# Tile loads issued from GpSimd's software DMA queue instead of SyncE's hardware queue

## The chip, the cores and the metric

The kernel runs on one core of one Trainium2 chip. The metric is device time in microseconds (us), as the median of several executions. Engines are named as in the profile: PE (TensorE), DVE (VectorE), ACT (ScalarE), POOL (GpSimd), SP (SyncE). A trailing q, as in SPq, is an engine's sequencer.

"The Trainium skill" is a set of notes on the chip. Where the text rests on it, it gives the page's title and section, and says whether the traces agree.

## The reference

Two independent decode attentions, A and B, each with 8 sequences, 32 heads, 4096 cached positions and head size 128, in bf16:

```python
def _A_ref(x, k_cache, v_cache, wq, wo):          # B is the same on its own inputs
    q = (x @ wq).reshape(8, 1, 32, 128).transpose(0, 2, 1, 3)
    scores = jnp.einsum("bhqd,bhkd->bhqk", q, k_cache) * (128 ** -0.5)
    p = softmax(scores, axis=-1)
    o = jnp.einsum("bhqk,bhkd->bhqd", p, v_cache)
    return o.transpose(0, 2, 1, 3).reshape(8, 1, 4096) @ wo
# result: concatenate([A, B], axis=-1)
```

There is one query per sequence, so every byte of the K and V caches is read once and used once: 1107 MB in all, with the weights.

## The kernel before

The work goes in 64 rounds, each over eight heads of one sequence: one K tile and one V tile of 8.39 MB each (128 partitions x 64 KB). Three such tiles fit in the on-chip memory: two slots take turns for K, the third holds V; the weights use the same slots at the start and the end. A load may be issued when the tile before it in its slot has been used.

```python
plan = [("wq", 0, 1), ("k", 0, 0), ("wq", 1, 2)]           # kind, number, slot
for n in range(NQ - 1):
    plan.append(("k", n + 1, (n + 1) % 2))
    plan.append(("v", n, 2))
plan += [("v", NQ - 1, NQ % 2), ("wo", 0, 2), ("wo", 1, (NQ - 1) % 2)]
...
def dma(out_ap, in_ap, key, deps, eng="sp"):               # loads go to SyncE
    return add(eng, lambda e: e.dma_start(out_ap, in_ap), deps, dma_key=key)
...
def load_tiles():
    while issued[0] < len(plan):
        kind, n, w = plan[issued[0]]
        prev = before[issued[0]]                           # the tile that held this slot
        dep = opUse.get(prev)                              # its last use, on PE
        if prev is not None and dep is None:
            return
        to, key = ring[:, w, :], ("t", w)
        if kind in ("k", "v"):
            ...
            opT[(kind, n)] = dma(to, from_, key, [dep])
        ...
        issued[0] += 1
```

In each quarter of a round, DVE multiplies a quarter of the K tile by the broadcast query, in place, and folds the halves of the head dimension. PE sums on, and DVE reduces the rest from PSUM:

```python
def make_mul(s):
    n = s // NR
    v = chunk(s).rearrange("p (t d) -> p t d", d=Dh)
    opMul[s] = add("dve", lambda e: e.tensor_tensor(
        v, v, qbc[:, n % 2, :].unsqueeze(1).to_broadcast([128, CT, Dh]), ALU.mult), [opT[("k", n)], opQbc[n]])
def make_fold(s):
    v = chunk(s).rearrange("p (t d) -> p t d", d=Dh)
    return add("dve", lambda e: e.tensor_tensor(v[:, :, 0:64], v[:, :, 0:64], v[:, :, 64:128], ALU.add), [opMul[s]])
```

The product with V of a round (`pv`, on PE) is done in the last two quarters of the following round; when it has ended, the next V load may be issued. The K slot comes free at the end of a round. GpSimd builds a few constants at the start (an identity, masks) and then does nothing.

Of the kernel before, what the change touches and what calls it, by code (L numbers as in the profile page):

```python
# [5 lines left out]
ALU = mybir.AluOpType  # L6
AX = mybir.AxisListType
# [24 lines left out]
class _Program:  # L32
# [11 lines left out]
    def add(self, eng, emit, deps=(), dma_key=None, moves=False):  # L44
        op = _Op(eng, emit, list(deps), dma_key, moves)
        if dma_key is not None:
            self.counts[dma_key] = self.counts.get(dma_key, 0) + 16
            op.token = (dma_key, self.counts[dma_key])
        for d in op.deps:
            if not (d.eng == "pe" and eng == "pe"):  # L50
                d.sig = True
        self.ops[eng].append(op)
        return op
# [86 lines left out]
def _build_kernel(nc, caches, out):  # L140
    B, Sq, D = caches[0][0].shape
    _, H, Sk, Dh = caches[0][1].shape
    NC = len(caches)
    assert B == 8 and Sq == 1 and Dh == 128 and Sk == 4096 and D == 1024 and H % 8 == 0 and 128 % H == 0
    DC = D // 128
    scale = float(Dh) ** -0.5
    HQ = 8
    MP = 128 // HQ
# [7 lines left out]
    PH = 128 // H  # L156
# [5 lines left out]
    with es:  # L162
# [5 lines left out]
        ident = sb("ident", [128, 128], BF16)  # L168
        own_m = sb("own_m", [128, HQ, PH], FP32)
        own_h = sb("own_h", [128, HQ], BF16)  # L170
        half = sb("half", [128, 2], FP32)
        E = sb("E", [128, 4, MB + PH - 1], BF16)
# [22 lines left out]
        proj = ps("proj")  # L195
# [10 lines left out]
        add = P.add  # L206

        def dma(out_ap, in_ap, key, deps, eng="sp"):
            return add(eng, lambda e: e.dma_start(out_ap, in_ap), deps, dma_key=key)


        def pool_select(view, base, pattern, dep, op=ALU.not_equal, fill=1.0, step=1):
            return add("pool", lambda e: e.affine_select(out=view, in_=view, compare_op=op, fill=fill,
                                                         base=base, pattern=pattern, channel_multiplier=step), [dep])
        c_ident = pool_select(ident[:], 0, [[-1, 128]], add("pool", lambda e: e.memset(ident[:], 0.0)))


        c_own = add("pool", lambda e: e.memset(own_m[:], 1.0))
        c_own = pool_select(own_m[:], 0, [[-MP, HQ], [0, PH]], c_own, ALU.is_ge, 0.0)
        c_own = pool_select(own_m[:], MP - 1, [[MP, HQ], [0, PH]], c_own, ALU.is_ge, 0.0, -1)  # L220
        own = own_m[:, :, 0]

        c_E = add("pool", lambda e: e.memset(E[:], 0.0))
        for q in range(4):
            c_E = pool_select(E[:, :, PH - 1:].rearrange("p i (j u) -> p i j u", u=PH)[:, :, :, 0], -32 * q, [[-8, 4], [-1, HQ]], c_E)
        c_oh = add("dve", lambda e: e.tensor_copy(own_h[:], own), [c_own])
        c_half = add("dve", lambda e: e.tensor_reduce(half[:], own.rearrange("p (g i) -> p i g", i=2), AX.X, ALU.add), [c_own])
        c_half = add("dve", lambda e: e.tensor_scalar(half[:], half[:], 1e30, -1e30, ALU.mult, ALU.add), [c_half])
        c_proj = add("dve", lambda e: e.memset(proj[:], 0.0))

        opT, opMul, opEacc, opRed, opNgm, opExp = {}, {}, {}, {}, {}, {}
        opPV, opAcc, opExt, opSt, opQb, opQbc, opQ, opQs, opQT = {}, {}, {}, {}, {}, {}, {}, {}, {}
        opOc, opNorm, opProj, opUse, opPM, opEv = {}, {}, {}, {}, {}, {}
        outs = []


        plan = [("wq", 0, 1), ("k", 0, 0), ("wq", 1, 2)]
        for n in range(NQ - 1):
# [11 lines left out]
        def where(n):  # L250

            return n // (B * HB), n // HB % B, n % HB
# [4 lines left out]
# [3 lines that stand above are left out]
                prev = before[issued[0]]  # L260
                dep = opUse.get(prev)
# [3 lines that stand above are left out]
                if kind in ("k", "v"):  # L265
                    c, b, hb = where(n)
                    from_ = caches[c][1 if kind == "k" else 2][b, hb * HQ:(hb + 1) * HQ].rearrange("u (m t) d -> (u m) (t d)", m=MP)
                    opT[(kind, n)] = dma(to, from_, key, [dep])
                elif kind == "wq":
                    opT[(kind, n)] = dma(to[:, 0:DC * H * Dh], caches[n][3].rearrange("(p k) n -> p (k n)", k=DC), key, [dep])  # L270
                else:
                    from_ = caches[n][4].rearrange("(p r) n -> p (r n)", r=H)
                    for i, (r0, r1) in enumerate(wo_cuts if n == NC - 1 else ((0, H),)):
                        opT[(kind, n, i)] = dma(to[:, r0 * D:r1 * D], from_[:, r0 * D:r1 * D], key if n < NC - 1 else ("w", i), [dep])
                issued[0] += 1


        def make_q(c):
            w = tile_of("wq", c)
            for f in range(2):  # L280
                def emit(e, f=f):
                    for k in range(DC):
                        for hb in range(HB):
                            col = k * H * Dh + (2 * hb + f) * 512
                            i = e.matmul(q_ps[f][32 * hb:32 * hb + B, :], xT[:, (c * DC + k) * B:(c * DC + k + 1) * B],  # L285
                                         w[:, col:col + 512], start=(k == 0), stop=(k == DC - 1), tile_position=(0, 32 * hb))
                    return i
                opQ[(c, f)] = add("pe", emit, [c_xT, opT[("wq", c)]] + [opQs.get((c - 1, hb, f)) for hb in range(HB)])
                for hb in range(HB):
                    rows = slice(32 * hb, 32 * hb + B)  # L290
                    opQs[(c, hb, f)] = add("act", lambda e, rows=rows, f=f: e.activation(q_sb[rows, c, f * 512:(f + 1) * 512], q_ps[f][rows, :], ACTF.Copy),  # L291
                                           [opQ[(c, f)]])
            opUse[("wq", c)] = opQ[(c, 1)]
# [153 lines left out]
        def emit_xT(e):  # L447
# [5 lines left out]
            return i  # L453
        op_xT = opUse[("x", 0)] = add("pe", emit_xT, [c_ident, op_x[-1]])
        load_tiles()
        c_xT = add("dve", lambda e: e.tensor_copy(xT[:], misc_bf16[:, 0:NC * DC * B]), [op_xT])
        make_q(0)
# [5 lines left out]
        for n in range(NQ):  # L463
            P.mark(n)
            for r in range(NR):
                s = n * NR + r
                make_mul(s)
                if s >= LAG:
                    make_red(s - LAG)
                if r == LAG - 1 and n >= 1:  # L470
                    make_shift(n - 1)
                fold = make_fold(s)
                if r == LAG - 1 and n >= 1:
                    make_pm(n - 1)
                if n == 0 and r == 1:
                    for c in range(1, NC):
                        make_q(c)
                        make_qT(c)
                if r == 2 and n >= 1:
                    make_pv(n - 1, 0, RG // 2)  # L480
                if r == 3 and n >= 1:
                    make_pv(n - 1, RG // 2, RG)
                    make_acc(n - 1)
                if r == 2 and n + 1 < NQ:
                    make_stage(n + 1)
                    make_qbc(n + 1)
                make_eacc(s, fold)
                load_tiles()
                if r == 3 and n >= 1:
                    make_ext(n - 1)  # L490
        P.mark(NQ)
        n = NQ - 1
# [4 lines left out]
        make_pv(n, 0, RG)  # L497
        make_acc(n)
        load_tiles()
        make_ext(n)  # L500
        make_norm(1)
# [31 lines left out]
def bass_concat_heads__mha_block_cached__mha_block_cached__decode_kernel(  # L533
    nc, A_x, A_k_cache, A_v_cache, A_wq, A_wo, B_x, B_k_cache, B_v_cache, B_wq, B_wo, out,
):
    caches = [(A_x, A_k_cache, A_v_cache, A_wq, A_wo), (B_x, B_k_cache, B_v_cache, B_wq, B_wo)]
    _build_kernel(nc, caches, out)
# [28 lines left out]
```

## Time and profile before

| before | value | view |
|---|---|---|
| time | 2566.66 us (3 runs), 2567.07 us with a fourth | runs |
| DMA share and rate, 500 to 2000 us | 1.00, 434 GB/s | windows |
| DVE busy | 85% of the span | page, part 1 |
| DVE idle per round, waiting for K | 4.8 us | waits |
| issue to landing, K and V | 40 us and 27.9 us | DMA issues |

The first fence is the windows view. Its columns are the stretch, its length, the busy time of PE, weight loads, DVE, ACT and POOL with instruction counts in brackets, the granted PE clock, the DMA share and GB/s.

```profile
110.00:150.00 40.00, 21.30 (x155) 7.50 (x154) 39.90 (x20) 2.14 (x7) 0.00 (x0) 0.74 0.99 420
500.00:1250.00 750.00, 328.04 (x2203) 115.17 (x2195) 652.13 (x308) 36.13 (x116) 0.00 (x0) 0.70 1.00 434
```

The stretch from 1250 to 2000 us has the same share and rate. The DMA engines are never idle in the steady part. A round moves 16.8 MB, which at 434 GB/s takes 38.7 us, and that is the length of a round. The next fence has two lines of the waits view: who waited for what, total us, times, longest.

```profile
DVE ring L330 <- DMA ring<-in_B_k_cache_dram: 153.3, 32, 4.8
DVE ring L330 <- DMA ring<-in_A_k_cache_dram: 150.0, 30, 9.7
```

Then two lines of the page: the DMA queue of the loads (packets, MB, share of the engines' span), and the chain of work that ended last.

```profile
q1 hardware_dynamic: 19344, 1107.32, 99.8%
...
DMA 51%; DVE 28%; issue 16%; PE 5%; another core or an unknown queue 0%; ACT 0%; DVEq 0%; SPq 0%
```

The loads make up nearly all traffic, and half of the chain. DVE stops once in every round, for the K tile. Its 85% hides that it isn't the limit. Now the timeline of one round (start, length, engine, line, operation, and in brackets the idle time before it):

```profile
1205.74 0.33 SPq L209 DMA_DIRECT2D ring<-in_A_k_cache_dram  x1
1207.02 4.42 DVE L330 TENSOR_TENSOR ring<-ring,qbc 128x8192 bf16<-128x8192 bf16 x1 [4.77 <-DMA ring<-in_A_k_cache_dram]
...
1237.11 0.33 SPq L209 DMA_DIRECT2D ring<-in_A_v_cache_dram  x1
1244.62 0.33 SPq L209 DMA_DIRECT2D ring<-in_B_k_cache_dram  x1
1245.74 4.42 DVE L330 TENSOR_TENSOR ring<-ring,qbc 128x8192 bf16<-128x8192 bf16 x1 [4.80 <-DMA ring<-in_A_k_cache_dram]
```

The K tile issued at 1205.7 lands at 1245.6, 40 us later, though its own transfer takes 19.3 us (8.39 MB at 434 GB/s). It stood in the queue behind a V tile. The V tile issued at 1237.1 stands behind that K tile. As long as each load is in the queue before the engines have finished the load ahead of it, the moment of its issue doesn't matter.

### The profile page before, as it was taken

To read this page: it belongs to the slowest core of one execution; us is meant where nothing else is said; L and a number is where in the kernel's file an instruction comes from. 1 tells how busy PE (TensorE), PEld (TensorE's weight loads), DVE (VectorE), ACT (ScalarE), POOL (GpSimd) and SP (SyncE) were. 2 spreads that over 40 slices of the span, in tenths; PEclk is the share of its full clock that TensorE was granted. 3 is DMA by queue.
4 is the path that set the end of the run, shared out by engine and by line. 5 is a ranking of instruction groups with operands and counts; after the bars stand their busy time and mean duration, and the time that the engine had idled before them with its cause. 6 is when DMAs were issued, how large, how long until landed. Compare 5 with 4: busy or idle time off the path is not lost.

```text
span 2565.3 us, 18707 instructions
## 1 busy us (share of the span) xinstructions
PE 1125.5 (44%) x7648; PEld 395.3 (15%) x7648; DVE 2172.4 (85%) x1043; ACT 130.0 (5%) x401; POOL 2.6 (0%) x14
## 2 busy tenths in 40 slices
PE   2543443444444444444444434444444434434435
PEld 0111111111111111111111111111111111111112
DVE  2898898898898898898888888988988988988983
ACT  1100000000000000000000000000000000000000
POOL 0000000000000000000000000000000000000000
PEclk7666667676766767767766767667766757667677
DMA  9999999999999999999999999999999999999998
GB/s 425 425 425 441 433 433 433 433 435 431 435 431 435 431 435 432 435 431 435 432 435 431 435 431 436 430 436 430 437 429 437 429 437 430 436 431 435 431 436 381
DMA packets 19435, 1107.51 MB, mean 432 GB/s; under 512 B 2209, under 2 KB 2257, under 8 KB 2401
## 3 DMA queue, kind: packets, MB, share of 16 engines
q1 hardware_dynamic: 19344, 1107.32, 99.8%
q8 instruction: 7, 0.11, 0.0%
q10 hardware_dynamic: 80, 0.05, 0.0%
q14 instruction: 4, 0.02, 0.0%
HBM read 1107.33 MB, written 0.03 MB: 432 GB/s over the span
## 4 chain that ended last, share of the span: by engine, by line
DMA 51%; DVE 28%; issue 16%; PE 5%; another core or an unknown queue 0%; ACT 0%; DVEq 0%; SPq 0%
DMA ring<-in_B_k_cache_dram 25%; DMA ring<-in_A_k_cache_dram 25%; DVE ring L330 10%; DVE ring L335 10%; PE red L345 4%; DVE s_sb L353 4%; DVE PM L370 3%; DMA ring<-in_B_wo_dram 1%; DVE rmax L359 1%; DVE rtmp L360 0%; PE proj L433 0%; ACT PM L291 0%; PE o L285 0%; DVEq L135 0%
## 5 line engine op out<-in xcount | busy, mean ns | idle before, releaser
L345 PE MATMUL red<-ring,ident 128*128 128x512 bf16 x2048 | 785.6, 553 | 1380.5 <-DVE ring L335 1380.5
L330 DVE TENSOR_TENSOR ring<-ring,qbc 128x8192 bf16<-128x8192 bf16 x256 | 1131.1, 4418 | 303.4 <-DMA ring<-in_B_k_cache_dram 153.3
L335 DVE TENSOR_TENSOR ring<-ring 128x4096 bf16<-128x4096 bf16 x256 | 581.4, 2271 | 0.0
L345 PEld LDWEIGHTS red<-ring,ident 128*128 128x128 bf16 x2048 | 239.7, 128 | 1833.6 <-DVE ring L335 1482.9
L353 DVE TENSOR_REDUCE s_sb<-red 128x64 f32<-128x1024 f32 x256 | 311.0, 1215 | 3.7 <-PE red L345 3.7
L382 PE MATMUL pv<-ring,PM 128*32 128x512 bf16 x4096 | 274.0, 415 | 4.6 <-DVE PM L370 4.6
L370 DVE TENSOR_TENSOR PM<-pe,own_h 128x2048 bf16<-128x2048 bf16 x64 | 146.1, 2283 | 0.7 <-ACT pe L365 0.7
L382 PEld LDWEIGHTS pv<-ring,PM 128*32 128x32 bf16 x4096 | 103.9, 104 | 189.0 <-issue 116.3
L319 ACT ACTIVATE qbc<-misc 128x128 bf16<-128x128 f32 x64 | 17.8, 278 | 1072.4 <-PE misc L317 1072.4
L365 ACT ACTIVATE pe<-s_sb,ngm 128x256 bf16<-128x256 f32 x64 | 32.5, 508 | 468.5 <-DVE ngm L363 468.5
L390 ACT ACTIVATE accS<-pv 128x512 bf16<-128x512 f32 x64 | 38.2, 597 | 349.0 <-PE pv L382 349.0
L399 PEld LDWEIGHTS o<-accS,E 128*32 128x32 bf16 x1024 | 31.3, 100 | 49.4 <-issue 48.2
L399 PE MATMUL o<-accS,E 128*32 128x32 bf16 x1024 | 38.1, 185 | 0.7 <-ACT accS L390 0.7
L405 ACT ACTIVATE o_sb<-o 32x32 f32 (+1 forms) x64 | 11.9, 186 | 454.4 <-PE o L399 453.8
L305 DVE COPY qT<-misc 128x64 bf16<-128x64 bf16 x8 | 3.5, 435 | 33.3 <-PE misc L301 33.3
L359 DVE TENSOR_REDUCE rmax<-s_sb 128x1 f32<-128x256 f32 x64 | 26.9, 420 | 2.2
L438 DVE CAST orow<-proj 40x512 bf16<-40x512 f32 (+1 forms) x2 | 1.1, 554 | 26.7 <-PE proj L433 26.7
L433 PE MATMUL proj<-ring,on_sb 128*8 128x256 bf16 (+1 forms) x192 | 15.2, 395 | 13.8 <-DMA ring<-in_A_wo_dram 8.7
L312 ACT ACTIVATE qst<-qT 128x128 bf16 (+1 forms) x64 | 18.7, 293 | 2.0 <-DVE qT L305 2.0
L360 DVE TENSOR_SCALAR rtmp<-half,rmax 128x32 f32<-128x32 f32 x64 | 15.4, 241 | 2.2
L285 PE MATMUL o<-ring,xT 128*8 128x512 bf16 x64 | 7.1, 621 | 20.0 <-DMA ring<-in_A_wq_dram 11.0
L363 DVE TRANSPOSE_TENSOR_REDUCE ngm<-rtmp 128x1 f32<-128x32 f32 x64 | 13.5, 211 | 2.2
(33 smaller groups left out, 74.4 us busy)
## 6 DMA issues: line engine op xcount, KB each, us to landing
ring<-in_B_wo_dram SPq DMA_DIRECT2D x1, 6144.0 KB, 35.0
ring<-in_B_wo_dram SPq DMA_DIRECT2D x1, 1536.0 KB, 38.3
ring<-in_A_k_cache_dram SPq DMA_DIRECT2D x32, 40.0
ring<-in_A_v_cache_dram SPq DMA_DIRECT2D x32, 27.9
ring<-in_B_k_cache_dram SPq DMA_DIRECT2D x32, 39.8
ring<-in_B_v_cache_dram SPq DMA_DIRECT2D x32, 27.9
ring<-in_B_wo_dram SPq DMA_DIRECT2D x1, 512.0 KB, 39.0
out_dram<-orow SPq DMA_DIRECT2D x2, 4.0 KB
```

The lines of the kernel that those rows point to most:

```text
L312: return e.activation(qst[:, n % 2, :].rearrange("p (j m) -> p j m", m=MP), from_.unsqueeze(2).to_broadcast([128, HQ, MP]), ACTF.Copy)
L319: opQbc[n] = add("act", lambda e: e.activation(qbc[:, n % 2, :], misc[:, 0:Dh], ACTF.Copy), [opQb[n], _at(opMul, NR * (n - 2) + NR - 1)])
L330: opMul[s] = add("dve", lambda e: e.tensor_tensor(v, v, qbc[:, n % 2, :].unsqueeze(1).to_broadcast([128, CT, Dh]), ALU.mult), [opT[("k", n ...
L335: return add("dve", lambda e: e.tensor_tensor(v[:, :, 0:64], v[:, :, 0:64], v[:, :, 64:128], ALU.add), [opMul[s]])
L345: i = e.matmul(dst, ident[:], v[:, g, :, j, :], start=(j == 0), stop=(j == 3))
L353: opRed[s] = add("dve", lambda e: e.tensor_reduce(s_sb[:, n % 2, r * CT:(r + 1) * CT], red_ps[s % 2][:, :].rearrange("p (t w) -> p t w", w ...
L359: m = add("dve", lambda e: e.tensor_reduce(rmax[:], s_sb[:, n % 2, :], AX.X, ALU.max), [opRed[NR * n + NR - 1]])
L365: opExp[n] = add("act", lambda e, at: e.activation(pe[:], s_sb[:, n % 2, :], ACTF.Exp, bias=ngm[:, n % 2:n % 2 + 1], scale=scale, accum_ou ...
L370: opPM[n] = add("dve", lambda e: e.tensor_tensor(PM[:], pe[:].unsqueeze(2).to_broadcast([128, T, HQ]), own_h[:].unsqueeze(1).to_broadcast( ...
L382: i = e.matmul(pv_ps[32 * q:32 * (q + 1), :], PM[:, t:t + 4, :].rearrange("p t j -> p (t j)"), v[:, t * Dh:(t + 4) * Dh], start=(g == 0), ...
L390: opAcc[n] = add("act", lambda e: e.activation(accS[:], pv_ps[:], ACTF.Copy), [opPV[n], _at(opExt, n - 1)])
L399: x = e.matmul(to, E[:, i, PH - 1 - u:PH - 1 - u + MB], accS[:, i * 128 + H * u:i * 128 + H * (u + 1)], start=(i == 0 and u == 0), stop=(i ...
```

## The change

The intent is to free SyncE of the tile loads and to use GpSimd, idle after its constants, as the issuing engine; so that its first two loads aren't held up, GpSimd issues them before it builds its constants. The diff, cut:

```diff
+        def tile_dma(out_ap, in_ap, key, deps):
+            return dma(out_ap, in_ap, key, deps, "pool")
...
-                    opT[(kind, n)] = dma(to, from_, key, [dep])
+                    opT[(kind, n)] = tile_dma(to, from_, key, [dep])
...   (the same for the wq and wo loads)
                 issued[0] += 1
-
+        load_tiles()
+
+        def pool_select(view, base, pattern, dep, ...):     # the constants, moved here from above
+        ...
```

Slots, order, waits and bytes are unchanged, and so are the instructions of PE, ACT and DVE. 132 loads (64 K, 64 V, four of weights, the last one in three pieces) make 134 issues.

More of the change, by code (lines that the diff above doesn't have):

```diff
@@ L209, in dma @@
             return add(eng, lambda e: e.dma_start(out_ap, in_ap), deps, dma_key=key)
-        def pool_select(view, base, pattern, dep, op=ALU.not_equal, fill=1.0, step=1):
-            return add("pool", lambda e: e.affine_select(out=view, in_=view, compare_op=op, fill=fill,
-                                                         base=base, pattern=pattern, channel_multiplier=step), [dep])
-        c_ident = pool_select(ident[:], 0, [[-1, 128]], add("pool", lambda e: e.memset(ident[:], 0.0)))
-        c_own = add("pool", lambda e: e.memset(own_m[:], 1.0))
-        c_own = pool_select(own_m[:], 0, [[-MP, HQ], [0, PH]], c_own, ALU.is_ge, 0.0)
-        c_own = pool_select(own_m[:], MP - 1, [[MP, HQ], [0, PH]], c_own, ALU.is_ge, 0.0, -1)
-        own = own_m[:, :, 0]
-        c_E = add("pool", lambda e: e.memset(E[:], 0.0))
-        for q in range(4):
-            c_E = pool_select(E[:, :, PH - 1:].rearrange("p i (j u) -> p i j u", u=PH)[:, :, :, 0], -32 * q, [[-8, 4], [-1, HQ]], c_E)
-        c_oh = add("dve", lambda e: e.tensor_copy(own_h[:], own), [c_own])
-        c_half = add("dve", lambda e: e.tensor_reduce(half[:], own.rearrange("p (g i) -> p i g", i=2), AX.X, ALU.add), [c_own])
-        c_half = add("dve", lambda e: e.tensor_scalar(half[:], half[:], 1e30, -1e30, ALU.mult, ALU.add), [c_half])
-        c_proj = add("dve", lambda e: e.memset(proj[:], 0.0))
+        def tile_dma(out_ap, in_ap, key, deps):
+            return dma(out_ap, in_ap, key, deps, "pool")
         opT, opMul, opEacc, opRed, opNgm, opExp = {}, {}, {}, {}, {}, {}
@@ L267, in load_tiles @@
                     from_ = caches[c][1 if kind == "k" else 2][b, hb * HQ:(hb + 1) * HQ].rearrange("u (m t) d -> (u m) (t d)", m=MP)
-                    opT[(kind, n)] = dma(to, from_, key, [dep])
+                    opT[(kind, n)] = tile_dma(to, from_, key, [dep])
                 elif kind == "wq":
-                    opT[(kind, n)] = dma(to[:, 0:DC * H * Dh], caches[n][3].rearrange("(p k) n -> p (k n)", k=DC), key, [dep])
+                    opT[(kind, n)] = tile_dma(to[:, 0:DC * H * Dh], caches[n][3].rearrange("(p k) n -> p (k n)", k=DC), key, [dep])
                 else:
@@ L273, in load_tiles, with pool_select @@
                     for i, (r0, r1) in enumerate(wo_cuts if n == NC - 1 else ((0, H),)):
-                        opT[(kind, n, i)] = dma(to[:, r0 * D:r1 * D], from_[:, r0 * D:r1 * D], key if n < NC - 1 else ("w", i), [dep])
+                        opT[(kind, n, i)] = tile_dma(to[:, r0 * D:r1 * D], from_[:, r0 * D:r1 * D], key if n < NC - 1 else ("w", i), [dep])
                 issued[0] += 1
+        load_tiles()
+        def pool_select(view, base, pattern, dep, op=ALU.not_equal, fill=1.0, step=1):
+            return add("pool", lambda e: e.affine_select(out=view, in_=view, compare_op=op, fill=fill,
+                                                         base=base, pattern=pattern, channel_multiplier=step), [dep])
+        c_ident = pool_select(ident[:], 0, [[-1, 128]], add("pool", lambda e: e.memset(ident[:], 0.0)))
+        c_own = add("pool", lambda e: e.memset(own_m[:], 1.0))
+        c_own = pool_select(own_m[:], 0, [[-MP, HQ], [0, PH]], c_own, ALU.is_ge, 0.0)
+        c_own = pool_select(own_m[:], MP - 1, [[MP, HQ], [0, PH]], c_own, ALU.is_ge, 0.0, -1)
+        own = own_m[:, :, 0]
+        c_E = add("pool", lambda e: e.memset(E[:], 0.0))
+        for q in range(4):
+            c_E = pool_select(E[:, :, PH - 1:].rearrange("p i (j u) -> p i j u", u=PH)[:, :, :, 0], -32 * q, [[-8, 4], [-1, HQ]], c_E)
+        c_oh = add("dve", lambda e: e.tensor_copy(own_h[:], own), [c_own])
+        c_half = add("dve", lambda e: e.tensor_reduce(half[:], own.rearrange("p (g i) -> p i g", i=2), AX.X, ALU.add), [c_own])
+        c_half = add("dve", lambda e: e.tensor_scalar(half[:], half[:], 1e30, -1e30, ALU.mult, ALU.add), [c_half])
+        c_proj = add("dve", lambda e: e.memset(proj[:], 0.0))
         def make_q(c):
```

## The prediction

> What bounds the kernel now: the tile loads. Between 500 and 2000 us the windows view shows a DMA share of 1.00 at 434 GB/s. One round (a K tile and a V tile, 16.8 MB) takes 38.7 us: the timeline has K loads issued at 1205.7, 1244.6 and 1282.1 us, and 16.8 MB at 434 GB/s is 38.7 us. DVE works 85% of the span and idles 4.8 us in every round, waiting for the K tile. The chain that ended last is 51% DMA. So a delayed issue counts only if the DMA engines run dry, or if the rate falls.
>
> What the change does. 134 issues leave SyncE's hardware queue for GpSimd's software queue. Waits, order, slots and bytes are the same, and so are the instructions of PE, ACT and DVE. GpSimd issues the first weight load and the first K load before its constants (2.55 us of work, between 0.8 and 4.1 us in the timeline).
>
> Costs.
> (1) Issue to first byte. SyncE spends 0.33 us on an issue. The Trainium skill ("DMA: Bandwidth & Descriptors", Specifications) gives about 1 us to the first byte on the software path, 0.6 us on the hardware path; no trace here shows it yet. My estimate is 1 to 2 us per load. In steady state it is hidden: a V load lands 27.9 us after its issue and needs 19.3 us of transfer (8.39 MB at 434 GB/s), so it is queued some 8 us early; a K load lands after 40 us, so some 20 us early. Only the first loads (1 to 2 us) and the tail (below 1 us) are exposed.
> (2) A starved descriptor generator. The Trainium skill ("SBUF — State Buffer", Who interferes with whom) says that GpSimd can be locked out of descriptor writing while VectorE runs a two-port instruction, but infers that tensor_tensor does not do that. DVE's long operations here are tensor_tensor (4.42, 2.27, 2.28 us), with reductions from PSUM (1.22 us) between them. Even one lockout would end after 4.4 to 6.7 us, under V's 8 us. Nothing on the critical path.
> (3) DVE held up by GpSimd: two issues per round of about 1 us, against 4.8 us of DVE idle. Nothing.
> (4) Rate. Each load is moved as 128 packets of 64 KB now (19344 packets for 1107 MB). If software makes the same rows, the rate stays 434 GB/s. If it cuts them finer or one DMA engine lags, every per cent of rate is about 25 us. That is the main risk.
> (5) Constants come 2 to 4 us later; the identity is first needed at 10.8 us, when x has landed. Nothing.
>
> Prediction: 2570 us, +0.1%: about 2 us at the start, 1 us at the end. Eight times in ten between 2563 and 2600. Faster by over 2%: 0.01 (the engines are already full). Within 2%: 0.88. Slower by over 2%: 0.11.
>
> What would show it. Right: a software queue with about 19300 packets, windows at 434 GB/s and share 1.00, DVE still waiting 4 to 5 us for each K tile, V landing after about 28 us, the first Q matmul at 23.5 to 26 us instead of 22.9. Wrong: more packets or a lower steady rate (step 4); a DMA share under 1.00 with V landing right after its transfer time (step 2); multiplies longer than 4.42 us, or DVE gaps that no DMA ends (step 3).
>
> What would make it wrong: finer descriptors, one slow DMA engine on the software queue, or software issues of many microseconds that eat V's 8 us.

## The result, and the profile after

The changed kernel takes 2567.48 us (2567.24 to 2568.58, 4 runs). The kernel before has 2567.07 us in the same rounds. The ratio is 1.0004, 95% interval 0.999 to 1.0018: the same. Ratios in this document are the mean time of one kernel's fast runs over that of the other's of the same rounds, so not quite the ratio of the medians quoted.

The lines of the profile after, first the windows:

```profile
110.00:150.00 40.00, 22.87 (x153) 7.70 (x152) 39.90 (x20) 2.14 (x7) 1.05 (x2) 0.70 0.95 402
500.00:1250.00 750.00, 334.55 (x2206) 115.78 (x2203) 652.30 (x308) 36.14 (x116) 21.09 (x40) 0.67 1.00 433
```

The steady rate is 433 GB/s against 434, from 1250 to 2000 us too. Only the ramp, 110 to 150 us, shows a difference: a share of 0.95 against 0.99. It costs nothing that shows: DVE's multiplies are 0.7 us later than before at 44 us, and 0.5 us later at 240 us. The waits view, as before:

```profile
DVE ring L332 <- DMA ring<-in_B_k_cache_dram: 153.1, 32, 4.8
DVE ring L332 <- DMA ring<-in_A_k_cache_dram: 149.4, 30, 9.8
```

The page's queue and chain:

```profile
q0 software_dynamic: 19296, 1107.30, 99.8%
...
DMA 51%; DVE 28%; issue 16%; PE 5%; another core or an unknown queue 0%; DVEq 0%; ACT 0%; POOL 0%; POOLq 0%
```

The software queue cuts the loads into the same packets: 19296 of them, plus the 48 of the result that stay on SyncE, are the 19344 of before. DVE waits as long for K as it did. The timeline of the same round:

```profile
1206.54 0.53 POOL L209 DMA_DIRECT2D ring<-in_A_k_cache_dram  x1 [6.71 <-PE red L347]
1207.63 4.43 DVE L332 TENSOR_TENSOR ring<-ring,qbc 128x8192 bf16<-128x8192 bf16 x1 [4.77 <-DMA ring<-in_A_k_cache_dram]
...
1237.99 0.53 POOL L209 DMA_DIRECT2D ring<-in_A_v_cache_dram  x1 [30.93 <-PE pv L384]
1245.50 0.53 POOL L209 DMA_DIRECT2D ring<-in_B_k_cache_dram  x1 [6.97 <-PE red L347]
1246.36 4.43 DVE L332 TENSOR_TENSOR ring<-ring,qbc 128x8192 bf16<-128x8192 bf16 x1 [4.81 <-DMA ring<-in_A_k_cache_dram]
```

And the page's DMA issues of V, with the median us from issue to landing:

```profile
ring<-in_A_v_cache_dram POOLq DMA_DIRECT2D x32, 27.6
```

From 1207 to 1246 us the whole round is shifted by 0.6 us and is otherwise the same: 38.7 us long, K issued 7.5 us after V, V landing 27.6 us after its record. A record on GpSimd is 0.53 us where SyncE's was 0.33. The timeline of the start has the first loads and, last, the first Q matmul:

```profile
1.32 0.66 POOL L209 DMA_DIRECT2D ring<-in_A_wq_dram  x1 [0.81 <-POOLq L553]
1.98 0.53 POOL L209 DMA_DIRECT2D ring<-in_A_k_cache_dram  x1
3.29 1.13 PE L453 MATMUL misc<-ident,ring 8*128 8x8 bf16 x16 [3.29 <-POOL ident L262]
23.67 3.58 PE L287 MATMUL o<-ring,xT 128*8 128x512 bf16 x32 [19.24 <-DMA ring<-in_A_wq_dram]
```

In the kernel before, the same places read:

```profile
0.81 0.41 SPq L209 DMA_DIRECT2D ring<-in_A_wq_dram  x1
10.77 1.10 PE L451 MATMUL misc<-ident,ring 8*128 8x8 bf16 x16 [10.77 <-DMA ring<-in_B_x_dram]
22.87 3.58 PE L285 MATMUL o<-ring,xT 128*8 128x512 bf16 x32 [11.00 <-DMA ring<-in_A_wq_dram]
```

The weight load was issued at 0.81 us and the same matmul began at 22.87, so the start is 0.8 us later. The transposes of x (the line at 3.29), on the other hand, begin at 3.29 us; before, they began at 10.77, with the idle time before them put down to the x loads. That gain buys nothing, because the Q matmul waits for the weights.

### The profile page after: what moved, and what is told of

Its sections match the earlier page's. It is cut to its first block, busy times and chain, and to the rows that moved or that the text cites. A ratio compares the mean times of both kernels' runs of the same rounds, so it can differ in the third digit from the quotient of the medians.

```text
span 2565.5 us, 18707 instructions
## 1 busy us (share of the span) xinstructions
PE 1123.8 (44%) x7648; PEld 394.8 (15%) x7648; DVE 2172.7 (85%) x1043; ACT 130.0 (5%) x401; POOL 73.4 (3%) x148
## 3 DMA queue, kind: packets, MB, share of 16 engines
q0 software_dynamic: 19296, 1107.30, 99.8%
## 4 chain that ended last, share of the span: by engine, by line
DMA 51%; DVE 28%; issue 16%; PE 5%; another core or an unknown queue 0%; DVEq 0%; ACT 0%; POOL 0%; POOLq 0%
DMA ring<-in_B_k_cache_dram 25%; DMA ring<-in_A_k_cache_dram 25%; DVE ring L332 10%; DVE ring L337 10%; PE red L347 4%; DVE s_sb L355 4%; DVE PM L372 3%; DMA ring<-in_B_wo_dram 1%; DVE rmax L361 1%; DVE rtmp L362 0%; PE proj L435 0%; PE o L287 0%; PE pv L287 0%; DVEq L135 0%
## 5 line engine op out<-in xcount | busy, mean ns | idle before, releaser
L332 DVE TENSOR_TENSOR ring<-ring,qbc 128x8192 bf16<-128x8192 bf16 x256 | 1131.8, 4421 | 302.5 <-DMA ring<-in_B_k_cache_dram 153.1
L209 POOL DMA_DIRECT2D ring<-in_A_v_cache_dram x32 | 16.9, 527 | 992.3 <-PE pv L384 952.5
L209 POOL DMA_DIRECT2D ring<-in_B_v_cache_dram x32 | 16.9, 528 | 968.5 <-PE pv L384 961.5
L209 POOL DMA_DIRECT2D ring<-in_A_k_cache_dram x32 | 16.9, 528 | 237.7 <-PE red L347 214.4
L209 POOL DMA_DIRECT2D ring<-in_B_k_cache_dram x32 | 16.9, 528 | 212.5 <-PE red L347 204.1
## 6 DMA issues: line engine op xcount, KB each, us to landing
ring<-in_A_k_cache_dram POOLq DMA_DIRECT2D x32, 39.6
ring<-in_A_v_cache_dram POOLq DMA_DIRECT2D x32, 27.6
ring<-in_B_v_cache_dram POOLq DMA_DIRECT2D x32, 27.6
```

Source lines behind the costliest of these rows:

```text
L332: opMul[s] = add("dve", lambda e: e.tensor_tensor(v, v, qbc[:, n % 2, :].unsqueeze(1).to_broadcast([128, CT, Dh]), ALU.mult), [opT[("k", n ...
```

## The experiments

The theory: the software queue is slower for each load, but the DMA engines are the limit and each load is queued before they come to it, so only the first load and the ramp show it. Rivals: the software queue costs nothing for each load, so there was nothing to hide; or the slack is so large that it never matters. A second question is whether DVE can lock GpSimd out of issuing. Eleven kernels were run, all against the kernel before.

### The cost of one load by itself: serial loads on both queues

Each load waits until the load before it has landed. No load is queued ahead, so every load shows its whole latency. The edit, cut, is the same in both kernels (with `dma` for `tile_dma` on SyncE):

```diff
                 to, key = ring[:, w, :], ("t", w)
+                after = [dep, last[0]]            # last[0]: the load issued before this one
...
-                    opT[(kind, n)] = tile_dma(to, from_, key, [dep])
+                    opT[(kind, n)] = tile_dma(to, from_, key, after)
...   (the same for the wq and wo loads; then last[0] is set to the load just issued)
```

> The kernel before, with each tile load made to wait until the load before it has landed, so nothing is queued early and each of 130 loads shows its whole latency from issue to first byte and from last byte to semaphore. Both theories expect slower: 2567 us + 130 x about 2.5 us (estimate from the first load, which took 22 us from issue to use against 19.3 us of transfer) = about 2890 us (2800 to 3000). Time from issue to landing should be one value near 22 us for every load.

> The changed kernel with the same serial loads. Theory 1 (the software queue is slower per load, and only the queueing ahead hides it): slower than the serial kernel on SyncE by 130 x 0.2 to 0.8 us, that is 25 to 100 us. Theory 2 (the software queue costs nothing per load, so there was nothing to hide): within 10 us of the serial kernel on SyncE.

Measured: 2904.00 us on SyncE (ratio to before 1.131) and 3005.63 us on GpSimd (1.1711). The difference of 101.6 us over 131 serial steps is 0.78 us per load. The software queue does cost more per load; the rival that it costs nothing is out. The timelines, first SyncE's, then GpSimd's, show where the 0.78 us lie:

```profile
1233.25 0.33 SPq L209 DMA_DIRECT2D ring<-in_A_v_cache_dram  x1
1233.31 4.43 DVE L333 TENSOR_TENSOR ring<-ring,qbc 128x8192 bf16<-128x8192 bf16 x1 [9.73 <-DMA ring<-in_A_k_cache_dram]
...
1255.03 0.33 SPq L209 DMA_DIRECT2D ring<-in_A_k_cache_dram  x1
```

```profile
1227.94 4.43 DVE L335 TENSOR_TENSOR ring<-ring,qbc 128x8192 bf16<-128x8192 bf16 x1 [11.21 <-DMA ring<-in_A_k_cache_dram]
1228.37 0.53 POOL L209 DMA_DIRECT2D ring<-in_A_v_cache_dram  x1 [22.18 <-DMA ring<-in_A_k_cache_dram]
...
1250.79 0.53 POOL L209 DMA_DIRECT2D ring<-in_A_k_cache_dram  x1 [21.89 <-DMA ring<-in_A_v_cache_dram]
```

Both DVE and the issuing engine wait for the same landed K tile. SyncE's record starts 0.06 us before DVE's multiply, GpSimd's 0.43 us after it: half a microsecond that the record of the software issue doesn't contain. From the start of the record to the landing, V takes 21.8 us on SyncE and 22.1 us on GpSimd (medians). So 0.5 us come before the record and 0.3 us after its start. The DMA packets in the two packed traces, which no view prints one by one, confirm this over all 128 K and V loads (medians). After the landing that it waited for, the next record starts 0.06 us later on SyncE and 0.54 us later on GpSimd. The first packet starts 0.95 us after the record on SyncE and 1.22 us on GpSimd. From there on the queues are alike: the packets take 20.5 us, and the landing comes 0.3 us after the last. From the end of the wait to the first packet this makes 1.0 us on SyncE and 1.8 us on GpSimd. From its first packet to the end of its last, a lone load thus takes 20.5 us, where a load in a full queue takes 19.3. The Trainium skill ("Perfetto Trace Analysis", DMA Instruction — SWDGE (GPSIMD)) says that such an instruction has no start marker, only an end. The profile here does show a start, but it lies 0.54 us after the landing, so it can't be taken for the moment at which the wait was over.

The 22.1 us are also about the shortest time in which a V load can land, since nothing is ahead of it. In the changed kernel V lands after 27.6 us, so its spare time is 5.5 us; K, landing after 39.6 us, has 17.5 us.

### Overdrawing the slack: GpSimd delayed before every V issue

Chained memsets on GpSimd, after V's wait and before its issue, 7 or 28 of them. GpSimd issues in order, so the K load behind that V is held back too. The edit, cut:

```diff
                 to, key = ring[:, w, :], ("t", w)
+                if kind == "v":
+                    for _ in range(7):            # 28 in the second kernel
+                        junk[0] = add("pool", lambda e: e.memset(orow[:], 0.0), [dep, junk[0]])
...   (the output copy, which uses orow, waits for the last memset)
```

> The changed kernel with seven chained GpSimd memsets before every V issue, estimated at 4 to 6 us in all. Theory 1 (a V load has about 8 us between issue and the time the engines come to it, of which some 2 us are its own latency, so about 6 us to spare): same time as the changed kernel within 0.3%, V landing some 5 us sooner after its issue (22 to 24 us). Rival (the issue path is on the critical path): 64 x 5 us = 320 us slower.

> The same with 28 memsets, estimated at 15 to 22 us. Theory 1: the slack of V is overdrawn and the DMA engines run dry. A round then lasts half of (V issue at 30 us into the round + delay + 2 us of latency + 38.7 us of transfer), because V(n), K(n+2) are paced by the round two before: for 18 us of delay 44 us against 38.7 us, so 2567 + 63 x 5.6 = about 2920 us (2750 to 3150), DMA share under 0.95 in steady windows, V landing 21 to 22 us after issue. Theory 2 (slack much larger than 8 us, since K is queued 20 us early): no change, 2567 us.

The seven memsets took 4.02 us, the 28 took 16.26 us. Measured: 2576.86 us (ratio 1.0039, interval 1.0022 to 1.0056) and 3036.44 us (1.1829).

The windows of the kernel with 4.02 us of delay:

```profile
110.00:150.00 40.00, 21.80 (x153) 7.49 (x152) 39.90 (x20) 2.15 (x7) 4.68 (x9) 0.71 0.89 381
500.00:1250.00 750.00, 334.61 (x2220) 116.07 (x2212) 652.74 (x309) 36.34 (x116) 93.25 (x180) 0.68 1.00 433
```

In the steady part the delay is swallowed: 64 times 4.02 us would be 257 us, and what came is 9 us. V lands 23.9 us after its issue, 1.8 us above the floor of 22.1, close to the 1.5 us that 5.5 less 4.0 leaves. But the expectation of under 0.3% was missed. In the ramp at 110 to 150 us, where the kernel hasn't built up its queue yet, the share falls to 0.89, against 0.95 in the changed kernel. By the round at 1207 us this kernel is 4.7 us late (its multiply starts at 1212.31), by 2446 us 6.0 us, and its profiled span ends 8.2 us later: a part in the ramp, a part in the last loads. The rest of the creep is not accounted for.

With 16.26 us the slack is gone. The windows line shows a share of 0.85, and the timeline what a round has become:

```profile
500.00:1250.00 750.00, 279.31 (x1816) 96.52 (x1816) 554.94 (x264) 30.67 (x99) 257.26 (x492) 0.62 0.85 362
```

```profile
1242.56 0.53 POOL L209 DMA_DIRECT2D ring<-in_A_v_cache_dram  x1
...
1264.65 3.45 PE L388 MATMUL pv<-ring,PM 128*32 128x512 bf16 x32 [4.98 <-DMA ring<-in_A_v_cache_dram]
...
1271.91 16.26 POOL L251 MEMSET orow<- 128x512 bf16 x28 [28.31 <-PE pv L388]
...
1288.12 0.53 POOL L209 DMA_DIRECT2D ring<-in_A_v_cache_dram  x1
```

The page's chain by line shows what ended last over the whole run:

```profile
POOL orow L251 30%; DMA ring<-in_B_v_cache_dram 23%; DMA ring<-in_A_v_cache_dram 23%; PE pv L388 11%; PE red L351 5%; DMA ring<-in_B_wo_dram 1%; DMA ring<-in_A_k_cache_dram 1%; DVE ring L336 1%; DVE ring L341 1%; PE misc L323 0%; DVE s_sb L359 0%; PE proj L439 0%; ACT PM L297 0%; PE o L291 0%
```

V now lands 22.1 us after its issue, at the floor. The expectation of about 2920 us for 18 us of delay was too low, though in its range. Its formula, half of a path through two rounds, gives 43.5 us a round for the 16.26 us of delay, and that path isn't what limited this kernel. The lines show a longer loop, with one turn in each round. The V load issued at 1242.56 us lands 22.1 us later. PE, which has waited 5 us for it, ends the product with V 7.3 us after that. Then the memsets take 16.26 us, and the next V load is issued at 1288.12. The turn leaves no gap between these parts, and the chain consists of the same three: V loads, memsets and PE (the 5% of `red` is work that PE does between the halves of the product). Over 45 such turns in the trace the means are 22.1, 7.8 and 16.3 us, 46.1 us in all. Against the 38.7 us of a round before, 63 rounds of 46.1 us are some 467 us longer; the measured difference to the changed kernel's median is 469 us. The rival of a boundless slack is out: the slack is finite. In this loop each us of delay costs a us in every round. Where between 4.02 and 16.26 us of delay the loss begins was not measured.

### Undoing one part: constants before the first loads

The call of `load_tiles()` is moved behind the constants.

> The changed kernel with the constants built before the first two loads are issued (one part of the change undone). Theory 1 (what is exposed is the start: every us by which the first load is late is a us of the whole): first Q matmul at 26 to 27 us instead of 23.7, whole time 2 to 3 us more, 2569 to 2571 us. Rival (the start is hidden too): 2567.5 us, first matmul unchanged.

Measured: 2570.97 us (5 runs), ratio 1.0016 (interval 1.0002 to 1.0029). The timeline of the start:

```profile
4.35 0.69 POOL L209 DMA_DIRECT2D ring<-in_A_wq_dram  x1 [0.27 <-issue]
26.96 3.58 PE L287 MATMUL o<-ring,xT 128*8 128x512 bf16 x32 [22.75 <-DMA ring<-in_A_wq_dram]
```

The first load is issued 3.0 us later than in the changed kernel, the first Q matmul starts 3.3 us later, the round at 1207 us 4.0 us later, and the profiled span is 3.9 us longer. The start is exposed, about one to one. Issuing the first two loads ahead of the constants is worth these 3 to 4 us; without it the software queue would have cost 0.16% instead of nothing that shows.

### Can DVE lock GpSimd out of issuing?

The Trainium skill ("SBUF — State Buffer", Who interferes with whom) says that VectorE in a two-port mode and GpSimd exclude each other, and infers that a tensor_tensor doesn't hinder descriptor writing. The serial kernel already answers for tensor_tensor. All V issues but the first and the last, 62 of 64, fall inside a 4.43 us multiply there, and the view of these issues shows no longer records (minimum, median, maximum in ns) and no later landing than K's (median 22.1 us too), which were all but seven issued while no multiply ran:

```profile
L209 POOL DMA_DIRECT2D ring<-in_A_v_cache_dram x32: 527/527/530, 94.3 to 1499.3; - x32
DMA to landing us min/median/max: 21.9/22.1/22.3
```

To see what a two-port operation does, the multiply was replaced by tensor_scalar passes over the same bf16 chunk; the page counts tensor_scalar among those that can run in a two-port mode. A pass takes 2.3 us for the same elements as the 4.42 us multiply.

```diff
-            opMul[s] = add("dve", lambda e: e.tensor_tensor(v, v, qbc[...], ALU.mult), ...)
+            for i in range(3 if r == NR - 1 else 2):
+                opMul[s] = add("dve", lambda e: e.tensor_scalar(v, v, 1.0, 0.0, ALU.mult, ALU.add),
+                               [opT[("k", n)], opQbc[n]] if i == 0 else [opMul[s]])
```

> The changed kernel with every tensor_tensor multiply of the K tile replaced by two (three in the last quarter, where the V load is issued) tensor_scalar passes over the same bf16 chunk, SBUF to SBUF, about 2.2 us each; the result is wrong on purpose. Lockout theory: a V issue that falls under such a pass can't write its descriptors, and its record on GpSimd grows from 0.53 us to somewhere up to 2.7 us, or V lands up to 2 us later after its issue than in the changed kernel (27.6 us). Theory of no lockout in this kernel whatever DVE runs: all issues stay at 0.53 us and V at 27 to 28 us. Both expect the time within 0.5% of 2567 us, since V has 4 us and more to spare.

> Control: the kernel before (loads on SyncE) with the same tensor_scalar passes in place of the multiply; wrong on purpose. Lockout of GpSimd as the cause of the long K issues on GpSimd (median 2.47 us): here every issue on SyncE stays at 0.33 to 0.43 us. Time: if the 4 us by which the two-pass kernel on GpSimd was slower come from the lockout, 2567 us here; if from the longer DVE rounds, 2571 us here too.

Measured: 2571.40 us on GpSimd (ratio 1.0016, interval 1.0001 to 1.0032) and 2569.90 us on SyncE (1.0014, interval 0.9997 to 1.0031). The timeline of the GpSimd kernel:

```profile
1199.12 6.94 DVE L333 TENSOR_SCALAR ring<-ring 128x8192 bf16<-128x8192 bf16 x3
1203.31 0.54 POOL L209 DMA_DIRECT2D ring<-in_A_v_cache_dram  x1 [28.40 <-PE pv L385]
...
1211.02 4.62 DVE L333 TENSOR_SCALAR ring<-ring 128x8192 bf16<-128x8192 bf16 x2 [1.63 <-DMA ring<-in_A_k_cache_dram]
1213.34 2.42 POOL L209 DMA_DIRECT2D ring<-in_A_k_cache_dram  x1 [9.49 <-PE red L348]
```

The K issue starts with the second of two passes and ends at 1215.76 us, 0.12 us after that pass ends (1211.02 + 4.62). Its record is 2.4 us instead of 0.53; over all K issues the median is 2.47 us. The V issue shown fell near the boundary of two passes and got away with 0.54 us, as did 63 of the 64; one took 2.39. On SyncE every issue stays at 0.33 us, but for one of 0.42. So the lockout exists, and it is bounded by the DVE instruction that is running. It cost no time that these runs resolve, since K, landing 36.3 us after its issue in this kernel, has 14 us to spare: the control on SyncE, whose issues aren't locked out, is as slow within the intervals. The 3 to 4 us that both lost go with the changed DVE work and weren't followed up.

What the lockout costs where nothing hides it comes from the serial kernels with the same passes:

> Serial loads on GpSimd plus the tensor_scalar passes, so that nothing hides a late issue; wrong on purpose. When a K tile lands, DVE starts its first pass (2.3 us) at once, and GpSimd comes to its V issue 0.4 us later. Lockout theory: each V issue waits for the end of that pass, record 1.9 to 2.1 us instead of 0.53, that is 1.4 to 1.6 us more for 63 V loads and perhaps some K loads: 3006 + 90 to 200 = about 3100 us (3090 to 3210). No lockout: 3006 us within 10.

> The same on SyncE, as control: 2904 us within 10 under either theory if DVE's passes matter only through GpSimd; near 3000 us if they slow the loads in some other way.

Measured: 3102.09 us on GpSimd, 2907.74 us on SyncE. Against the serial kernels with the multiply that is 96.5 us more on GpSimd (3005.63) and 3.7 us more on SyncE (2904.00). The timeline on GpSimd:

```profile
1220.29 4.62 DVE L336 TENSOR_SCALAR ring<-ring 128x8192 bf16<-128x8192 bf16 x2 [9.62 <-DMA ring<-in_A_k_cache_dram]
1220.71 1.99 POOL L209 DMA_DIRECT2D ring<-in_A_v_cache_dram  x1 [21.98 <-DMA ring<-in_A_k_cache_dram]
```

The V issue starts 0.42 us into the first pass and ends at 1222.70 us, 0.1 us after its end (half of 4.62 us after 1220.29). The record has grown by 1.46 us, and V lands 23.5 us after its start instead of 22.1. 62 of the 64 V records have grown so, by 90 us together, and three other records by 4 us: that is 94 of the 96.5 us, and the control on SyncE lost 3.7 us without any of it. The same page of the skill (A bandwidth-pool intuition that's wrong) gives "blocked until DVE-end + ~115 ns". The trace agrees: all 64 K and V records that grew in this kernel end 0.12 us after the end of a pass.

### Many small loads on both queues

Each K and V tile is loaded by 64 DMAs of 128 KB (1 KB per partition), spread over four semaphores per slot:

```diff
-                    opT[(kind, n)] = tile_dma(to, from_, key, [dep])
+                    for i in range(64):
+                        cut = slice(i * T * Dh // 64, (i + 1) * T * Dh // 64)
+                        last[i % 4] = tile_dma(to[:, cut], from_[:, cut], (("t", "u1", "u2", "u3")[i % 4], w), [dep])
...   (the multiply and the product with V wait for all four semaphores; SyncE's kernel has dma for tile_dma)
```

> The kernel before with every K and V tile loaded by 64 DMAs of 128 KB (1 KB per partition) on SyncE instead of one of 8 MB, spread over four semaphores per slot. Issue cost read from the traces, back to back: 0.43 us on SyncE (three issues in 1.28 us), so 64 issues take 27 us per tile against 19.3 us of transfer; 128 issues per round = 55 us, 64 rounds = about 3500 us (3400 to 4200). If the issue were no limit on SyncE, 2567 us or whatever 1 KB rows cost the engines.

> The changed kernel cut in the same way, on GpSimd. Theory 1 (the issue of a software DMA takes GpSimd 0.52 us, back to back, whatever its size): 128 issues per round = 67 us, 64 rounds = about 4300 us (4200 to 5000), some 20 to 25% slower than the same cut on SyncE. Theory 2 (software issues overlap or are cheaper for small rows): equal to the cut kernel on SyncE or faster.

Measured: 3993.09 us on SyncE (ratio 1.556), 4380.04 us on GpSimd (1.7078). The timelines, first SyncE's, then GpSimd's:

```profile
2019.66 30.54 SPq L209 DMA_DIRECT2D ring<-in_B_k_cache_dram  x64
```

```profile
2002.10 33.75 POOL L209 DMA_DIRECT2D ring<-in_A_k_cache_dram  x64
```

The queue and chain of GpSimd's kernel, from its page:

```profile
q0 software_dynamic: 394080, 1107.82, 80.1%
...
POOL 99%; DMA 1%; PE 0%; issue 0%; DVE 0%; POOLq 0%
```

Here the issue is the limit. GpSimd is in the chain for 99% of the span, and 64 issues take it 33.75 us, 0.527 us each, the same as for a load of 8 MB. 64 rounds of 2 x 33.75 us are 4320 us of the 4380. So the issue costs GpSimd 0.53 us per DMA at both sizes, and not by the byte. GpSimd was only 10% slower than SyncE, not the 20 to 25% expected: SyncE's 64 issues take 30.54 us, 0.477 us each, where three issues in the kernel before had suggested 0.43. Whether SyncE itself is slower there or is held by DMA engines that are 90% busy with 1 KB rows (GpSimd's kernel: 80%), these runs don't tell.

## Why the prediction was right

The measured 2567.5 us lie 2.5 us under the predicted 2570 and inside the range, and "within 2%" came true. Whether the changed kernel is slower at all, by the 0.4 us between the medians, the interval doesn't tell. Point by point:

1. What bounds the kernel. Right: the DMA share stayed at 1.00 and DVE's wait at 4.8 us in each round. Making the loads serial or V late enough, on either count, made the kernel 13 to 18% slower; a delay of 4 us on each V made it 0.4% slower.
2. Issue to first byte, "1 to 2 us per load", hidden but for the start and the tail. The mechanism was right. The term was rightly sized: from the end of the wait to the first packet a software load takes 1.8 us, SyncE's 1.0, and what the software queue adds over SyncE is 0.78 us for a whole load. The start was charged with 2 us and cost 0.8, since SyncE's first load has most of that latency too and only the difference is new (first packet at 2.68 us of the span against 1.86); the end was charged with 1 us and cost nothing that shows, as the profiled spans differ by 0.2 us. The Trainium skill ("DMA: Bandwidth & Descriptors", Specifications) gives about 1 against 0.6 us to the first byte, a difference of 0.4 us. The first packets here start 1.8 and 1.0 us after the end of the wait, a difference of 0.75 us, and the measurement decides.
3. "Queued some 8 us early." This was the loose step. 8 us is the landing time less the transfer, and it contains the load's own latency. The spare time of V is 5.5 us. The lockout of "4.4 to 6.7 us" that was called safe under 8 us would thus not have been safe at its upper end. It made no difference, because no tensor_tensor here locked GpSimd out of issuing, which no run had shown when the prediction was made, and with passes of 2.3 us the longest record seen is 2.6 us.
4. Starved descriptor generator: right for this kernel, and shown. In the serial kernel 62 V issues ran under a multiply, none longer than 0.53 us; in the changed kernel itself no K or V record is longer than 0.54 us. It holds only because the long DVE operations are tensor_tensor; with tensor_scalar passes GpSimd was locked out.
5. DVE held up by GpSimd: right. The multiply takes 4421 ns in the mean, against 4418.
6. Rate, named as the main risk: it didn't come. The packets are the same 19344, the rate is 433 against 434 GB/s.
7. Later constants: right that they cost nothing. Not foreseen was that the x rows land some 7 us sooner. The first Q matmul came at 23.67 us, within the predicted 23.5 to 26.

No version in these runs beats the kernel before, and at a DMA share of 1.00 there was nothing for the issuing engine to win.

## What to carry to other kernels

In a kernel limited by DMA, the issuing engine matters only through what is left of each load's lead: take the time from issue to landing, and subtract not the transfer but the landing time of a load with nothing ahead of it. Here moving the loads to the software queue costs 0.78 us per load, which a lead of 5.5 us swallows in steady state, and which shows only at the first load. Keep the loads on the hardware queue if they are many and small (GpSimd needed 0.53 us per DMA at 128 KB as at 8 MB; with 128 KB the whole kernel was 10% slower than on SyncE), if they aren't queued ahead, or if DVE runs long tensor_scalar passes from on-chip memory to on-chip memory; and issue the first load before anything else on its engine.

## What the Trainium skill lacked or had wrong

- "SBUF — State Buffer", Who interferes with whom, marks as inferred that tensor_tensor doesn't hinder descriptor writing. Shown here: 62 issues of 0.527 to 0.530 us, all inside tensor_tensor multiplies of 4.43 us with two on-chip inputs. The lockout by tensor_scalar passes, which the page counts among the possible two-port operations, and its end 0.12 us after a pass, agree with the page.
- "DMA: Bandwidth & Descriptors", Specifications, gives about 1 against 0.6 us to the first byte. Here the first packet starts 1.8 against 1.0 us after the end of the wait (1.22 against 0.95 us after the start of the record). It doesn't say what a whole load costs more on the software queue: 0.78 us per serial load, of which 0.5 us lie before the shown record.
- The same page, Bandwidth, has 79.0 us for a load of 16 MB beside 425 GB/s, which don't fit together. Here a load of half that size took 22.1 us from issue to landing on the software queue, and back-to-back loads ran at 433 GB/s.
- No page has what a software issue costs GpSimd, back to back: 0.527 us, the same for 128 KB and for 8 MB.
- The same page, SWDGE vs HWDGE vs iDMA, says that a packet is preferably at most 4096 bytes. For 1 KB rows this agrees on the software queue: 394080 packets in all, 48 for each of the 8192 DMAs of 128 rows (32 of 4096 bytes and 16 of 4 bytes), where SyncE's queue made 1180560, with each row a packet of 1 KB. For 64 KB rows a packet is a whole row of 65536 bytes on both queues, which that section doesn't say.
